# The last FFN products of a retention and maxout kernel by one level of Strassen's algorithm, from the second token tile on

## The chip, the cores and the metric

The kernel runs on one core of a Trainium2 chip. The metric is device time in microseconds (us) of one execution; medians are of several executions. The profile is of one execution; times in it count from its span's start. The engines are TensorE (PE for matmuls, PEld for its weight loads), VectorE (DVE), ScalarE (ACT), GpSimd (POOL) and SyncE (SP, which here issues the transfers). PSUM is the memory that TensorE writes its results to. The granted clock is the share of TensorE's full clock that the chip's throttle let through.

## The reference

```python
scores = (1 / sqrt(D)) * q @ k.transpose(0, 1, 3, 2)     # 8 batches, 8 heads, 576 tokens, D = 64
out    = (scores * Dmat) @ v                              # Dmat: decay gamma**(i-j), lower triangle
x      = out.transpose(0, 2, 1, 3).reshape(4608, 512)
h      = maximum(maximum(x @ w1, x @ w2), x @ w3)         # 512 -> 768
return (h @ w_out).astype(float32)                        # 768 -> 512
```

Everything is computed in float32; the weights come as float64 and are converted on the chip.

## The kernel before

Tokens go in nine tiles of 512. While the feed-forward of tile t runs, the attention of tile t+1 is computed in four chunks of three steps each (transposes, scores, values); a step stands between any two pieces of feed-forward work. A tile has nine "up" units, for three pairs fp of 128-column blocks of h and three weight matrices i, and then the last layer, called "down". From tile 1 on the up units already use one level of Strassen's algorithm (Winograd's form): seven products of half size in place of eight, with sums of the blocks made beforehand. Down is plain:

```python
def up(t, h, fp, i):                        # seven products, 4 instructions each
    product(1, x, True);  p1 = kept("p1", x)            # kept: ScalarE copy out of PSUM
    ...
    product(5, x, False)
    nc.vector.tensor_tensor(c22, x[:], p7[:], op=ALU.add)      # L343, frees bank x for product 3
    ...
    product(3, x, False)
    ...                                                        # i > 0:
        nc.vector.tensor_tensor(h[:, f1, lo], h[:, f1, lo], x[:], op=ALU.max)        # L354
        nc.vector.tensor_tensor(h[:, f0, :], h[:, f0, :], ..., op=ALU.max)           # L355

def down(t, h, m):
    ps = ps_y.tile([P, DM], FP32, tag="y", name="down")
    for fb in range(NF):                                       # NF = 6
        nc.tensor.matmul(ps[:], lhsT=h[:, fb, m * P:(m + 1) * P], rhs=w_sb["out", fb][:],
                         start=(fb == 0), stop=(fb == NF - 1))
    osb = opool.tile([P, DM], FP32, tag="osb", name="osb")
    nc.scalar.copy(osb[:], ps[:])
    nc.sync.dma_start(out[...], osb[:])

def ffn(t):
    for n, (fp, i) in enumerate(units):
        ...                                                    # up (tile 0: plain)
            if t == 1:
                weight_sums(n + 2)                             # sums of w1..w3, made during tile 1
        yield                                                  # an attention step runs here
    for m in range(NT // P):                                   # 4 row blocks
        down(t, h, m)
        ...
```

## Time and profile before

| | before |
|---|---|
| time, median of 3 runs | 861.55 us (860.62 to 861.91) |
| span of the profiled run | 857.7 us |
| mean granted TensorE clock | 0.998 |
| TensorE matmuls busy | 844.4 us, 98% |
| VectorE busy | 393.6 us, 46% |
| GpSimd busy | 143.3 us, 17% |

TensorE is the bound; VectorE is idle for more than half of the span.

### The profile page before, as it was taken

Reading aid. Unit: us, or ns where it says so; the run is one execution under the profiler, and the core shown is the slowest. Engines: PE = TensorE matmul, PEld = TensorE weight load, DVE = VectorE, ACT = ScalarE, POOL = GpSimd, SP = SyncE. Lnnn points to the kernel's source line nnn. Section 1 sums busy time; section 2 is a strip of 40 time slices with the busy share of each in tenths; the row PEclk is TensorE's granted clock in tenths of the full one; section 3 lists DMA queues with packets and bytes.
Section 4 is the critical chain, followed back from the end, with each engine's and each line's share of the span. In section 5 each row is a group of like instructions: output and inputs, shape, how many; then the busy total and the mean of one; then the engine's idle time right before and its main releaser. Section 6 shows DMA issues by size and latency. Waiting matters only on the chain.

```text
span 857.7 us, 11778 instructions
## 1 busy us (share of the span) xinstructions
PE 844.4 (98%) x4320; PEld 614.0 (72%) x4320; DVE 393.6 (46%) x705; ACT 171.4 (20%) x367; POOL 143.3 (17%) x128
## 2 busy tenths in 40 slices
PE   7999989999999999999999999999999999999998
PEld 5645546887588758885788668875888588857883
DVE  4899945654244523444254335442544235432330
ACT  2565631111111102110111111111111011101211
POOL 3534423221210120102011111101111102100000
PEclk9999999999999999999999999999999999999999
DMA  9655531334133323332233213341333223200001
GB/s 245 173 151 160 181 70 43 55 57 85 43 54 56 55 66 66 54 56 61 47 64 68 57 49 56 55 85 45 56 56 54 66 52 66 44 26 24 1 1 49
DMA packets 228409, 59.01 MB, mean 69 GB/s; under 512 B 213504, under 2 KB 222720, under 8 KB 228352
## 3 DMA queue, kind: packets, MB, share of 16 engines
q1 hardware_dynamic: 227920, 57.74, 29.9%
q8 instruction: 34, 0.56, 0.3%
q10 hardware_dynamic: 432, 0.53, 0.2%
q14 instruction: 23, 0.19, 0.1%
HBM read 48.76 MB, written 9.44 MB: 68 GB/s over the span
## 4 chain that ended last, share of the span: by engine, by line
PE 87%; DVE 6%; ACT 4%; issue 1%; DMA 1%; SPq 1%; POOL 0%; DVEq 0%; ACTq 0%
PE x L315 29%; PE down L361 21%; PE z L315 14%; PE y L315 7%; PE s L178 4%; PE o L208 4%; PE o L213 3%; PE kv L189 3%; ACT expo L267 2%; ACT expo L271 1%; DVE expo L275 1%; DVE expo L264 1%; DVE h L375 1%; DVE st L181 1%; DMA kraw<-in_k_dram 1%
## 5 line engine op out<-in xcount | busy, mean ns | idle before, releaser
L361 PE MATMUL down<-wout,h 128*128 128x512 f32 x432 | 190.7, 594 | 3.0 <-POOL wout L278 3.0
L361 PEld LDWEIGHTS down<-wout,h 128*128 128x128 f32 x432 | 80.6, 190 | 95.9 <-issue 90.6
L315 PE MATMUL x<-S,T 128*128 128x256 f32 x576 | 147.9, 379 | 0.0
L148 POOL TENSOR_TENSOR vd<-vraw,gk 128x512 f32<-128x512 f32 x36 | 38.7, 1076 | 499.5 <-DMA vraw<-in_v_dram 483.6
L315 PEld LDWEIGHTS x<-S,T 128*128 128x128 f32 x576 | 109.1, 190 | 15.4 <-ACT u L320 0.3
L181 DVE TENSOR_TENSOR st<-s,causal 128x512 f32<-128x512 f32 x72 | 46.3, 685 | 65.6 <-PE s L178 65.6
L315 PE MATMUL x<-xT,w 128*128 128x256 f32 x288 | 74.8, 382 | 0.0
L315 PE MATMUL x<-S,w 128*128 128x256 f32 x288 | 74.4, 381 | 0.1
L315 PE MATMUL z<-xT,T 128*128 128x256 f32 x288 | 74.0, 379 | 0.0
L315 PE MATMUL z<-S,w 128*128 128x256 f32 x288 | 73.9, 379 | 0.0
L315 PE MATMUL y<-xT,w 128*128 128x256 f32 x288 | 73.9, 379 | 0.0
L320 ACT COPY p<-x 128x256 f32<-128x256 f32 x72 | 26.8, 373 | 220.8 <-PE x L315 217.8
L343 DVE TENSOR_TENSOR tmp<-x,p 128x256 f32<-128x256 f32 x48 | 20.4, 425 | 104.4 <-PE x L315 104.4
L364 ACT COPY osb<-down 128x512 f32<-128x512 f32 x36 | 21.1, 586 | 219.7 <-PE down L361 212.4
L370 PE MATMUL up<-xT,w 128*128 128x512 f32 x144 | 63.5, 594 | 0.4 <-DVE xT L215 0.4
L315 PEld LDWEIGHTS z<-S,w 128*128 128x128 f32 x288 | 54.7, 190 | 7.4
L315 PEld LDWEIGHTS y<-xT,w 128*128 128x128 f32 x288 | 54.7, 190 | 7.4
L315 PEld LDWEIGHTS z<-xT,T 128*128 128x128 f32 x288 | 54.0, 189 | 8.4 <-ACT p L320 0.3
L315 PEld LDWEIGHTS x<-S,w 128*128 128x128 f32 x288 | 49.4, 189 | 13.4 <-issue 1.3
L315 PEld LDWEIGHTS x<-xT,w 128*128 128x128 f32 x288 | 51.5, 190 | 9.6 <-issue 4.2
L215 DVE TENSOR_TENSOR xT<-o,gq 128x512 f32<-128x512 f32 x36 | 24.8, 690 | 69.7 <-PE o L213 63.8
L370 PEld LDWEIGHTS up<-xT,w 128*128 128x128 f32 x144 | 26.7, 190 | 30.9 <-issue 30.1
(64 smaller groups left out, 867.8 us busy)
## 6 DMA issues: line engine op xcount, KB each, us to landing
bits<-in_moe_w_dram SPq DMA_DIRECT2D x18, 512.0 KB, 3.6
out_dram<-osb SPq DMA_DIRECT2D x36, 256.0 KB, 2.0
kraw<-in_k_dram SPq DMA_DIRECT2D x32, 256.0 KB, 3.0
vraw<-in_v_dram SPq DMA_DIRECT2D x32, 256.0 KB, 3.5
qraw<-in_q_dram SPq DMA_DIRECT2D x448, 16.0 KB, 1.9
kxraw<-in_k_dram SPq DMA_DIRECT2D x448, 16.0 KB, 1.8
bits<-in_moe_w_out_dram SPq DMA_DIRECT2D x6, 512.0 KB, 3.5
qraw<-in_q_dram SPq DMA_DIRECT2D x7, 256.0 KB, 4.6
```

The lines of the kernel that those rows point to most:

```text
L148: nc.gpsimd.tensor_tensor(t[:], raws.pop(("v", g))[:], gk[:].unsqueeze(2).to_broadcast([C, H, D]), op=ALU.mult)
L178: nc.tensor.matmul(s[j][:, p, :], lhsT=kT[r, p, :], rhs=qT[r, p, :], start=True, stop=True)
L181: nc.vector.tensor_tensor(st[:, j], s[j][:], masks[start_of(g)][:].unsqueeze(1).to_broadcast([C, NP, C]), op=ALU.mult)
L189: nc.tensor.matmul(kv[:, p, :], lhsT=pair(kr, p)[r:], rhs=pair(vds[g], p)[r:], start=True, stop=True)
L208: nc.tensor.matmul(o[D * j:D * (j + 1), p, :], lhsT=vr[:, 2 * p + j, :], rhs=st[:, j, p, :], start=(p == 0), stop=(old == 0 and p == NP - ...
L213: nc.tensor.matmul(o[:, p, :old], lhsT=sd[:, p, :], rhs=qT[:, p, :old], start=False, stop=(p == NP - 1), skip_group_check=True)
L215: nc.vector.tensor_tensor(xT[t][:, :, i * C:(i + 1) * C], o[:], gq[:], op=ALU.mult)
L315: nc.tensor.matmul(out[:], lhsT=w[:, d * P:(d + 1) * P], rhs=xS[t][n][:, d, :], start=first and d == 0, stop=d == 1, skip_group_check=True)
L320: nc.scalar.copy(c[:], src[:])
L361: nc.tensor.matmul(ps[:], lhsT=h[:, fb, m * P:(m + 1) * P], rhs=w_sb["out", fb][:], start=(fb == 0), stop=(fb == NF - 1))
L364: nc.scalar.copy(osb[:], ps[:])
L370: nc.tensor.matmul(ps[:], lhsT=w_sb[i, fb][:, dc * P:(dc + 1) * P], rhs=xT[t][:, dc, :], start=(dc == 0), stop=(dc == NDC - 1))
```

## The change

The last layer gets the same scheme. From tile 1 on it is seven products of (2 row blocks) × (3 pairs fp) matmuls with 256 columns. The sums of w_out are made once (`sums_of_outs`), behind unit 2 of tile 1. The sums of h are made per pair fp (`sums_of_hidden`) behind the unit that finishes the pair, which is unit 2, 5 or 8. The memory of the weight conversion is freed for them. The diff, cut to its core:

```diff
+    def sums_of_outs():
+        while_converting.close()
+        ...
+        nc.vector.tensor_tensor(t1, b12, b11, op=ALU.subtract)      # 128 x 768
+        nc.vector.tensor_tensor(t2, b22, t1, op=ALU.subtract)
+        nc.gpsimd.tensor_tensor(b12, b22, b12, op=ALU.subtract)
+        nc.gpsimd.tensor_tensor(t4, b21, t2, op=ALU.subtract)
+    def sums_of_hidden(h, fp):
+        ...
+        nc.vector.tensor_tensor(s1, a21, a22, op=ALU.add)           # 128 x 256
+        nc.vector.tensor_tensor(s2, s1, a11, op=ALU.subtract)
+        nc.gpsimd.tensor_tensor(s3, a11, a21, op=ALU.subtract)
+        nc.gpsimd.tensor_tensor(s4, a12, s2, op=ALU.subtract)
+    def downs(t, h):
+        def product(n, out, first):
+            for m in range(NM):                                     # NM = 2
+                for fp in range(NF // 2):                           # 3
+                    nc.tensor.matmul(out[:, m, :], lhsT=hS[n](fp)[:, m * P:(m + 1) * P],
+                                     rhs=late["T"][n][:, fp, :], start=..., stop=...)
+        ...                                     # products 1, 2, 6, 7, 5, 4, 3 as in up
@@ ffn
                 if t == 1:
                     weight_sums(n + 2)
+                if i == 2:
+                    if t == 1 and fp == 0:
+                        sums_of_outs()
+                    sums_of_hidden(h, fp)
             yield
+        if t == 0: ...                          # plain down
+        else:
+            for n, _ in enumerate(downs(t, h)): ...
```

## The prediction

> **What bounds the kernel now.** I read the page first: engine shares, then the chain that ended last, then the costliest groups.
>
> ```profile
> PE 844.4 (98%) x4320; PEld 614.0 (72%) x4320; DVE 393.6 (46%) x705; ACT 171.4 (20%) x367; POOL 143.3 (17%) x128
> PE 87%; DVE 6%; ACT 4%; issue 1%; DMA 1%; SPq 1%; POOL 0%; DVEq 0%; ACTq 0%
> L361 PE MATMUL down<-wout,h 128*128 128x512 f32 x432 | 190.7, 594 | 3.0 <-POOL wout L278 3.0
> L361 PEld LDWEIGHTS down<-wout,h 128*128 128x128 f32 x432 | 80.6, 190 | 95.9 <-issue 90.6
> L315 PE MATMUL x<-S,T 128*128 128x256 f32 x576 | 147.9, 379 | 0.0
> ```
>
> TensorE is busy 98% of the span and is 87% of the chain, so a TensorE instruction taken out of tiles 1 to 8 shortens the kernel one for one, unless a new wait eats it. The busy times of groups can't be added (pipelined matmuls of neighbouring groups overlap), so the cost of a matmul must come from starts. Two stretches of the last tile, where no attention is left, give it. First the chain, then the timeline around the last product of the last unit:
>
> ```profile
> 833.59 20.61 PE down L361 x48
> ```
>
> ```profile
> 831.70 1.03 PE L315 MATMUL z<-xT,T 128*128 128x256 f32 x4
> ...
> 832.56 1.03 PE L315 MATMUL x<-S,w 128*128 128x256 f32 x4
> ...
> 833.42 20.76 PE L361 MATMUL down<-wout,h 128*128 128x512 f32 x48
> ...
> 833.63 0.42 DVE L354 TENSOR_TENSOR h<-h,x 128x256 f32<-128x256 f32 x1
> ...
> 833.97 0.68 DVE L355 TENSOR_TENSOR h<-h,tmp 128x512 f32<-128x512 f32 x1
> ```
>
> A last-layer ("down") tile is 24 matmuls, which the trace shows as 48 instructions (an fp32 matmul is two), 20.61/48 = 0.429 us each at 512 columns. A Strassen product of the up layers (4 instructions of 256 columns) starts 0.86 us after the one before it: 832.56 − 831.70 = 0.86, 833.42 − 832.56 = 0.86, so 0.215 to 0.216 us each. Half the columns cost half the time: **the narrow matmul has almost no fixed cost**, since the weight load (190 ns) just fits under it. That is why Strassen pays at all here.
>
> The same lines show something that helps the old order and will not help the new one. The maximum that finishes the last pair of blocks of h (L355) ends at 833.97 + 0.68 = 834.65, 1.23 us after the first down matmul started. The old loop does not need that pair before its ninth instruction, 8 × 0.429 = 3.43 us in.
>
> **What the Trainium skill says.** (1) "TensorE: Matmul & The Clock Gate", Back-to-back issue gap: N/2.4 + 2.5 ns warm, 216 ns at 512 and 109 ns at 256. The trace has twice that for fp32 (429 and 216 ns), in the same proportion; I use the trace. (2) The same page, LDWEIGHTS: P/1.2, 107 ns for 128 columns; the trace says 190 ns, which leaves only 26 ns under a 216 ns matmul. (3) "SBUF — State Buffer", Who interferes with whom: a VectorE instruction with two SBUF inputs contends with a GpSimd instruction that reads SBUF. The trace agrees: L290 (256 columns) takes 0.41 us alone and 0.94 us beside GpSimd. (4) "Perfetto Trace Analysis", Tensor Engine Instruction: ends of TensorE instructions are estimates; hence my use of starts.
>
> **The change part by part.**
>
> *Matmuls.* Seven products × 2 row blocks × 3 pairs = 42 matmuls, 84 instructions of 256 columns. An up unit (28 such) repeats every 6.04 us in the last tile, so 84 take 3 × 6.04 = 18.12 us against 20.61 us. The gain is **2.49 us a tile, 19.9 us over eight tiles (2.3% of 861.55)**. Tile 0 keeps the old products. The weight loads rise from 48 to 84 a tile and stay hidden.
>
> *Evictions.* Out go four ScalarE copies of 512 (586 ns each, L364). In come six copies of 256 (373 ns), one of 512 on ScalarE, and six additions of 256 on VectorE (425 ns). A product now lasts 12 × 0.216 = 2.59 us, and each bank is next written one product later; two copies (0.75 us) or two additions (0.85 us) end well inside that. The up layers do the same with 0.86 us products and hardly ever wait. **Cost on the path: zero.** The output is the same bytes in four transfers; the tail (copy, transfer) I take as at most 0.3 us longer.
>
> *First product waits for h.* Product 1 takes fp = 0, 1, 2 in turn for its first row block, so it needs the last pair after 4 instructions: 4 × 0.216 = 0.86 us, not 3.43. In the last tile it would load at once but for L355: that ends at 834.65, the load then starts some 0.05 us later and its matmul 0.11 us after that (as in the wait shown below), at 834.81, where 833.42 + 0.86 = 834.28 was its turn. **0.53 us lost.** In the other tiles only two VectorE transposes stand between the last unit and product 1, nothing on TensorE, so the loss is the same: 8 × 0.53 = 4.2 us.
>
> *Sums of h.* Per pair of blocks: two VectorE and two GpSimd operations of 256 columns, three times a tile, right behind L355. They are not on TensorE, but VectorE works in order, and behind units 2 and 5 it then has the attention transposes (0.70 + 0.66) before it may serve unit 3 or 6. The trace has one case where exactly this queue stopped TensorE (tile 1, unit 3, where weight sums take the place of the new ones):
>
> ```profile
> 161.01 1.22 DVE L355 TENSOR_TENSOR h<-h,tmp 128x512 f32<-128x512 f32 x1
> 162.15 0.94 DVE L290 TENSOR_TENSOR T<-w,w 128x256 f32<-128x256 f32 x1
> 163.12 0.83 DVE L291 TENSOR_TENSOR T<-w,T 128x256 f32<-128x256 f32 x1
> 163.88 0.70 DVE L159 STREAM_TRANSPOSE kT<-kxraw 128x512 f32<-128x512 f32 x1
> 164.51 0.66 DVE L159 STREAM_TRANSPOSE qT<-qraw 128x512 f32<-128x512 f32 x1
> 165.10 0.38 DVE L333 TENSOR_TENSOR h<-y,p 128x256 f32<-128x256 f32 x1
> 165.41 0.40 DVE L343 TENSOR_TENSOR h<-x,p 128x256 f32<-128x256 f32 x1
> ...
> 165.86 0.73 PEld L315 LDWEIGHTS x<-S,w 128*128 128x128 f32 x4 [0.46 <-DVE h L343]
> ```
>
> L343 must empty x before product 3 writes it. How much room it has elsewhere is its idle time before it. In tile 7:
>
> ```profile
> 711.01 1.42 DVE L355 TENSOR_TENSOR h<-h,tmp 128x512 f32<-128x512 f32 x1
> ...
> 714.50 0.42 DVE L343 TENSOR_TENSOR h<-x,p 128x256 f32<-128x256 f32 x1 [0.55 <-PE x L315]
> ```
>
> Over tiles 2 to 7 that room in unit 3 is 1.84, 1.09, 1.16, 1.15, 0.94 and 0.55 us, and in unit 6 always 1.84 (1.01 in tile 1). It is small where a value scaling on GpSimd (L148, L195) lands on L355. My estimate for the new pair of sums is between 0.42 + 0.42 alone and 0.94 + 0.83 contended: 1.4 us. Beyond the room that leaves 0, 0.3, 0.25, 0.25, 0.45, 0.85 in unit 3 and 0.4 in unit 6 of tile 1: 2.5 us in all. The last tile has no transposes and loses none.
>
> *Sums of w_out, once.* They enter that same full queue in tile 1 before unit 3, where there is no room left. VectorE does two of 768 columns: from 0.41 us at 256 and 0.68 us at 512, about 0.95 us alone, the second about 1.9 us beside GpSimd. Adding the first sums of h (1.7 us contended) gives 4.5 us. **All of it should stop TensorE: 4.5 us.**
>
> *Sum.* 861.55 − 19.9 + 4.2 + 2.5 + 4.5 + 0.3 = 853.15, say **853.2 us**, 1.0% less.
>
> **The rivals.** (a) *Nothing is lost*: VectorE is only 46% busy, the sums vanish in idle time, all 19.9 us arrive: 841.7 us, faster by 2.3%. For it: the up layers run this scheme with almost no wait. Against it: the h dependency of product 1 is visible in starts, and VectorE's spare time is not where it is needed. (b) *VectorE's queue becomes the bound behind units 2, 5 and the down phase*: contention doubles all sums and GpSimd's own delays the decayed values and states. Were each of some 24 places to lose 0.8 us, the gain would be gone: about 861 us. The room of 1.84 us in unit 6 speaks against it. (c) *The weight load becomes the bound*: at 190 of 216 ns, if loads of the new layout slipped to 230 ns, 672 instructions × 14 ns = 9 us more, 862. The up layers already load from SBUF tiles of the same form at 216 ns, so I doubt it. (d) *The output transfers on the one in-order queue hold back the loads of q and k*: they are issued in the same order, and the last one now comes earlier, so no.
>
> **Range and chances.** The matmul gain is firm to about 0.5 us; the losses could be 4 to 18 us. So 848.0 to 858.5 us eight times in ten. Faster by 2% needs under about 844.5, thus losses under 3 us, less than product 1's wait alone: 5%. Slower by 2% would need 37 us of new waits: 1%.
>
> **What would show it.** The page should have no L361 down rows but tile 0's 48, and new product rows of 256 columns with starts 0.216 us apart. The waits of TensorE and its loads should list the last maximum of h ahead of product 1 (eight times about half a microsecond), and L343's counterpart ahead of product 3 in unit 3 of tile 1 (4 to 5 us) and, smaller, of tiles 3 to 7. VectorE busy should rise by some 50 to 60 us, ScalarE by some 4 (8 × (6 × 0.373 + 0.586 − 4 × 0.586) = 3.8). The prediction is wrong if product 1 doesn't wait, if the sums run without contention, or if starts in the new products are further apart than 0.216 us.

## The result

| | before | changed |
|---|---|---|
| time, median of 4 runs | 861.73 us (860.62 to 862.91) | 858.55 us (857.14 to 859.74) |
| ratio | | 0.9962 (0.9942 to 0.9982) |
| span of the profiled run | 857.7 us | 855.4 us |
| mean granted TensorE clock, profiled run | 0.998 | 0.991 |

A ratio is the mean time of one kernel's runs over that of the other's runs of the same rounds, so it is not quite the ratio of the medians quoted. The change is faster by 0.4%, within 2%, where 1.0% had been expected (853.2 us, in a range up to 858.5).

The page of the changed kernel, the engine shares, the granted clock in 40 slices and the chain that ended last by engine:

```profile
PE 831.4 (97%) x4608; PEld 669.8 (78%) x4608; DVE 448.2 (52%) x803; ACT 172.8 (20%) x391; POOL 189.4 (22%) x178
...
PEclk9999999989999999999999999999999999999999
...
PE 79%; DVE 8%; SPq 5%; ACT 4%; issue 3%; DMA 1%; POOL 0%; DVEq 0%
```

TensorE is busy 13 us less, but the span is only 2.3 us shorter. TensorE's share of the chain is down from 87% to 79%, and one slice of the clock row, the ninth (171 to 192 us), is no longer a 9. That slice lies in tile 1. (SyncE's 5% of the chain is an effect of how it is followed back: from transposes that queue behind the sums it goes to a transfer. VectorE's instructions stand back to back there, so no transfer held it up, and in e5 below the share is 1%.) To see where the expected gain went, compare starts of the same matmuls in the two traces:

| stretch | before | changed | difference |
|---|---|---|---|
| tile 1: product 3 of unit 2 to product 3 of unit 3 | 6.26 us | 13.00 us | +6.74 |
| tile 1: product 3 of unit 3 to product 1 of unit 4 | 3.15 us | 5.88 us | +2.73 |
| tile 1: product 3 of unit 2 to first down matmul | 45.15 us | 55.25 us | +10.1 |
| first down matmul of tile 1 to the end of the span | 652.95 us | 640.48 us | −12.5 |

So from the down phase of tile 1 on, the change earns 12.5 us, near what was expected, and **one stretch of tile 1 gives 10.1 us of it back**. Here it is, in the timeline of the changed kernel (columns: start, us, engine, line, operation; in brackets how long the engine had stood idle and what ended it). L322 and L323 are VectorE's sums of h, L312 and L313 its sums of w_out, L314 and L315 GpSimd's; L434 was L343 before, and L446 was L355.

```profile
164.01 1.48 DVE L312 TENSOR_TENSOR To<-w_out 128x768 f32<-128x768 f32 x1
...
165.52 1.36 DVE L313 TENSOR_TENSOR To<-w_out,To 128x768 f32<-128x768 f32 x1
166.03 2.51 POOL L314 TENSOR_TENSOR w_out<-w_out 128x768 f32<-128x768 f32 x1
...
166.81 2.02 DVE L322 TENSOR_TENSOR H<-h 128x256 f32<-128x256 f32 x1
168.51 1.98 POOL L315 TENSOR_TENSOR To<-w_out,To 128x768 f32<-128x768 f32 x1
168.86 1.90 DVE L323 TENSOR_TENSOR H<-H,h 128x256 f32<-128x256 f32 x1
...
172.22 0.40 DVE L434 TENSOR_TENSOR h<-x,p 128x256 f32<-128x256 f32 x1
...
172.67 2.08 PE L406 MATMUL x<-S,w 128*128 128x256 f32 x4 [6.80 <-DVE h L434]
...
174.68 2.08 PE L181 MATMUL s<-qT,kT 64*128 64x128 f32 x16
...
178.55 1.07 PE L406 MATMUL x<-xT,w 128*128 128x256 f32 x4
```

Two things are to be seen. First, VectorE's two sums of 256 columns took 2.02 and 1.90 us, and they end 0.29 and 0.27 us after the GpSimd instruction that ran beside each (166.81 + 2.02 = 168.83 against 166.03 + 2.51 = 168.54, and so on): each sat through GpSimd's. The same pair usually takes 0.42 and 0.83 us. VectorE is in order, so the transposes and then L434 come late, and TensorE stands for 6.80 us. Second, what TensorE does after the wait is slow as well: four matmuls take 2.08 us on record instead of 1.13, sixteen score matmuls 2.08 instead of 1.16. The same three groups in the kernel before:

```profile
165.86 1.13 PE L315 MATMUL x<-S,w 128*128 128x256 f32 x4
166.92 1.16 PE L178 MATMUL s<-qT,kT 64*128 64x128 f32 x16
...
169.01 1.03 PE L315 MATMUL x<-xT,w 128*128 128x256 f32 x4
```

The granted clock of the stretch from 170 to 180 us is 0.57. Asked in steps of 1 us, the trace has it at one half from 168.4 us, 2.5 us into the wait, to 178.6 us: 10.2 us in all, of which TensorE worked the last 6. (In every kernel here, the one before too, there is one more such fall, of 3.4 us, in tile 0. In the kernel before it begins at 117.3 us, behind waits of 1.10 and 1.90 us for converted weights. It is why the mean there is 0.998 and not 1.)

The other predicted wait, ahead of the last pair in product 1, is there in each of eight tiles (tile 1 shown):

```profile
214.92 1.03 PE L342 MATMUL dx<-w_out,h 128*128 128x256 f32 x4
...
215.46 0.69 DVE L446 TENSOR_TENSOR h<-h,tmp 128x512 f32<-128x512 f32 x1
...
216.20 1.99 PE L342 MATMUL dx<-w_out,h 128*128 128x256 f32 x8 [0.25 <-DVE h L446]
```

The second group's turn was 214.92 + 4 × 0.216 = 215.78. Its record starts with its weight load at 216.20, and the matmul itself 0.11 us later: 0.53 us late.

### The profile page after: what moved, and what is told of

Its sections match the earlier page's. It is cut to its first block, busy times and chain, and to the rows that moved or that the text cites. A ratio compares the mean times of both kernels' runs of the same rounds, so it can differ in the third digit from the quotient of the medians.

```text
span 855.4 us, 12581 instructions
## 1 busy us (share of the span) xinstructions
PE 831.4 (97%) x4608; PEld 669.8 (78%) x4608; DVE 448.2 (52%) x803; ACT 172.8 (20%) x391; POOL 189.4 (22%) x178
## 4 chain that ended last, share of the span: by engine, by line
PE 79%; DVE 8%; SPq 5%; ACT 4%; issue 3%; DMA 1%; POOL 0%; DVEq 0%
PE x L406 26%; PE z L406 12%; PE dx L342 9%; PE y L406 6%; PE dz L342 5%; PE s L181 4%; SPq L141 4%; PE o L211 4%; PE o L216 3%; PE kv L192 3%; PE dy L342 2%; PE down L452 2%; ACT expo L271 2%; ACT expo L275 1%; DVE expo L279 1%
## 5 line engine op out<-in xcount | busy, mean ns | idle before, releaser
L406 PE MATMUL x<-S,w 128*128 128x256 f32 x288 | 76.2, 387 | 8.6 <-DVE h L434 8.5
L434 DVE TENSOR_TENSOR tmp<-x,p 128x256 f32<-128x256 f32 x48 | 20.4, 425 | 104.8 <-PE x L406 104.8
L324 POOL TENSOR_TENSOR H<-h 128x256 f32<-128x256 f32 x24 | 22.7, 947 | 150.3 <-DVE h L446 150.3
L181 PEld LDWEIGHTS s<-qT,kT 64*128 64x128 f32 x576 | 37.2, 198 | 13.9 <-issue 11.4
L424 DVE TENSOR_TENSOR tmp<-y,p 128x256 f32<-128x256 f32 x48 | 20.4, 425 | 51.7 <-PE y L406 51.7
```

The source lines that it names most:

```text
L181: nc.tensor.matmul(s[j][:, p, :], lhsT=kT[r, p, :], rhs=qT[r, p, :], start=True, stop=True)
L406: nc.tensor.matmul(out[:], lhsT=w[:, d * P:(d + 1) * P], rhs=xS[t][n][:, d, :], start=first and d == 0, stop=d == 1, skip_group_check=True)
```

## The experiments

Theory A, formed from the two traces: three separate waits of TensorE ate the gain. They are the one-off sums of w_out in VectorE's full queue (with GpSimd holding VectorE up, and with a clock that falls during the wait), the wait of product 1 for the last pair of h, and the sums of h ahead of the transposes. Rivals: the sums cost the same wherever they stand; the lower clock comes from the denser narrow matmuls; the narrow products are themselves slower than taken. All seven runs gave correct results and were timed in five rounds against the kernel before.

| run | median us | kernel before | ratio (95% interval) |
|---|---|---|---|
| changed kernel | 858.55 | 861.73 | 0.9962 (0.9942 to 0.9982) |
| e1_outs_late | 851.28 | 861.83 | 0.9882 (0.9868 to 0.9896) |
| e2_gpsimd_part_late | 856.71 | 861.83 | 0.9948 (0.9934 to 0.9961) |
| e3_pair_last | 854.33 | 861.83 | 0.9918 (0.9903 to 0.9933) |
| e4_hidden_later | 851.03 | 861.83 | 0.9871 (0.9853 to 0.9889) |
| e5_all_three | 841.41 | 861.34 | 0.9765 (0.9752 to 0.9778) |
| e6_filled_wait | 856.53 | 861.34 | 0.9939 (0.9927 to 0.9951) |
| e7_sums_only | 872.78 | 861.04 | 1.0138 (1.0121 to 1.0155) |

The stretches of tile 1 from the profiled runs, as in the table above:

| run | unit 2 product 3 to unit 3 product 3 | unit 3 product 3 to unit 4 | unit 2 product 3 to first down matmul |
|---|---|---|---|
| before | 6.26 | 3.15 | 45.15 |
| changed | 13.00 | 5.88 | 55.25 |
| e1_outs_late | 8.00 | 3.14 | 47.47 |
| e2_gpsimd_part_late | 10.49 | 5.77 | 52.58 |
| e3_pair_last | 12.94 | 5.88 | 55.22 |
| e4_hidden_later | 9.18 | 4.76 | 49.68 |
| e5_all_three | 6.48 | 3.15 | 45.37 |
| e6_filled_wait | 12.75 | 3.15 | 52.23 |
| e7_sums_only | 12.85 | 5.89 | 55.37 |

e3 and e7 leave the queue of tile 1 as the change made it, and both repeat its delay: it is not a chance of one execution.

### e1_outs_late: the one-off sums behind unit 7

```diff
     def sums_of_outs():
-        nc.vector.tensor_tensor(t1, ...); nc.vector.tensor_tensor(t2, ...)
-        nc.gpsimd.tensor_tensor(b12, ...); nc.gpsimd.tensor_tensor(t4, ...)
+        def rest(): ...                     # the same four
+        late["rest"] = rest
@@ ffn, t == 1
+                    if n == 7:
+                        late["rest"]()
```

> The four one-off sums of w_out move from behind unit 2 of tile 1 to behind unit 7, where no weight sums and no attention transposes stand in VectorE's queue. Theory A (the one-off sums block VectorE's queue, TensorE waits 6.8 us ahead of product 3 of unit 3 and then runs some 3 us at half clock): the first down matmul of tile 1, 10.1 us later than in the kernel before, comes within 2 us of it, the granted clock is back at 0.998, and the time falls by 8 to 9.5 us to about 849 to 850.5. Rival B (the sums cost VectorE and GpSimd the same wherever they stand, the wait only moves to product 3 of unit 8 or to the first down products): a fall of under 3 us. Rival C (the lower clock comes from the denser narrow matmuls, not from the wait): the clock stays near 0.991 and the fall is about 7 us.

Measured: 851.28 us, 7.3 us less than the changed kernel, a little under the expected 8 to 9.5; the first down matmul comes 47.47 − 45.15 = 2.3 us late, not within 2. The time alone would fit rival C too; the clock decides. It is 0.998 in the profiled run and the stretch after unit 3 is 3.14 us again (three of the four executions have 0.998; the slowest, 852.41 us, has 0.996 and no trace). At the new place VectorE's two sums look like this in the timeline:

```profile
201.61 0.95 DVE L314 TENSOR_TENSOR To<-w_out 128x768 f32<-128x768 f32 x1
...
202.59 0.96 DVE L315 TENSOR_TENSOR To<-w_out,To 128x768 f32<-128x768 f32 x1
```

They cost 1.9 us instead of 2.8, and TensorE's list of waits has none for them: the same four instructions, in another place, are free. Rival B falls. So does rival C: the products are as dense as before and the clock is back. What the expectation had overlooked is that the sums of h of pair 0 still stand behind unit 2 among the weight sums, so that unit 3 keeps a delay of 8.00 − 6.26 = 1.74 us.

### e2_gpsimd_part_late: only GpSimd's half moved

```diff
         nc.vector.tensor_tensor(t1, ...); nc.vector.tensor_tensor(t2, ...)
-        nc.gpsimd.tensor_tensor(b12, ...); nc.gpsimd.tensor_tensor(t4, ...)
+        def rest(): ...                     # GpSimd's two, called at n == 7
```

> Only GpSimd's two one-off sums (768 columns, 2.5 and 2.0 us) move to behind unit 7; VectorE's two stay behind unit 2. Theory A1 (VectorE's first two sums of h took 2.0 and 1.9 us instead of 0.42 and 0.83 because GpSimd's two sums held the reads): those two fall to about 0.9 and 0.8 us, TensorE's wait from 6.8 to about 4.3 us, the time by 2.5 us if the clock still drops and up to 5 us if it does not. Rival (the queue is long because of its own VectorE work, contention is a detail): the wait stays above 6 us and the time within 1 us of the changed kernel.

In the timeline, the two sums of h (L326 and L327 here) and the matmul that waited:

```profile
169.39 0.94 DVE L326 TENSOR_TENSOR H<-h 128x256 f32<-128x256 f32 x1
170.37 0.42 DVE L327 TENSOR_TENSOR H<-H,h 128x256 f32<-128x256 f32 x1
...
172.75 2.07 PE L410 MATMUL x<-S,w 128*128 128x256 f32 x4 [4.28 <-DVE h L438]
```

They fall from 3.92 to 1.36 us together, and the wait from 6.80 to 4.28 us: 2.5 us, as expected of theory A1 (of the two sums, the second fell further than expected: to 0.42 us, not 0.8). **GpSimd's two sums made VectorE's two sums of h 2.5 us longer.** The clock still dropped (for 6.8 us, and the stretch after the wait is 5.77 us), and the time fell by 1.8 us. That is under the expected 2.5, but the intervals of the two ratios overlap; the stretches of the trace are the firmer measure here.

### e3_pair_last: the last pair of blocks last in each product

```diff
         def product(n, out, first):
-            for m in range(NM):
-                for fp in range(NF // 2):
+            for fp in range(NF // 2):
+                for m in range(NM):
```

> Down products take fp in the outer loop and the row block in the inner, so that the last pair of blocks of h is needed after 8 instructions of 0.216 us (1.73 us) instead of 4 (0.86 us). Theory A: the maximum that finishes that pair ends 1.23 us after the first down matmul, so the wait of about half a microsecond ahead of product 1 goes in all eight tiles: 4 us less, about 854.5. Rival (TensorE waits the same time a little later in product 1, or the order of writes to the bank costs time): within 1 us of the changed kernel.

Measured: 854.33 us, 4.2 us less, and the wait of product 1 for L446 is gone from the list of waits. The 0.53 us × 8 of the prediction is confirmed, by an edit that swaps two lines.

### e4_hidden_later: the sums of h behind units 3 and 6

```diff
                 if i == 2:
                     ...
-                    sums_of_hidden(h, fp)
+                    if fp == NF // 2 - 1:
+                        sums_of_hidden(h, fp)
+                if n in (3, 6):
+                    sums_of_hidden(h, n // 3 - 1)
```

> The sums of h of pairs 0 and 1 move from behind units 2 and 5 (full queue: maxima, then attention transposes) to behind units 3 and 6, which end without maxima and are followed by attention scores. Theory A: the waits ahead of product 3 of unit 3 in tiles 3 to 7 and of unit 6 in tile 1 (about 2 us together) go, and in tile 1 the wait behind unit 2 falls from 6.8 to about 3 us[...]: 2 + 3.8 + 2.6 = about 8 us less in all, 850. Rival (the sums are cheap, only the one-off sums matter): the tiles after the first gain nothing, and the time falls by what tile 1 gains alone.

Measured: 851.03 us, 7.5 us less. The waits of matmuls ahead of product 3 in tiles 2 to 7 are gone but for one of 0.17 us (tile 7, unit 0), which the changed kernel has too, and in tile 1 one of 2.95 us is left. One part of the expectation missed: I had taken a wait of 3 us to be too short for the clock to drop (the 2.6 us of the sum are the clock's). In the profiled execution it did drop, for 3.4 us:

```profile
171.58 1.96 PE L406 MATMUL x<-S,w 128*128 128x256 f32 x4 [2.95 <-DVE h L434]
...
173.47 1.95 PE L181 MATMUL s<-qT,kT 64*128 64x128 f32 x16
```

The five timed runs fall into two kinds: 848.43 and 849.09 us with a mean clock of 0.998, and 851.03 to 852.20 us with 0.993 to 0.996. That looks as if the drop came in three of five executions and cost some 2 to 3 us, but only one of them has a trace, and why the same wait should let the clock drop in some executions only is not shown.

### e5_all_three: the three edits together

The edits of e1, e3 and e4 in one kernel.

> The three edits together: one-off sums behind unit 7, last pair of h last in each down product, sums of h of pairs 0 and 1 behind units 3 and 6. Theory A (three separate waits on TensorE, which add up): from 858.55, 7.3 less for the first, 4.2 less for the second, and for the third the 5.6 us of waits ahead of product 3 that the first run alone left: about 841.5, faster than the kernel before by 2.3 to 2.4%, close to the full worth of the matmuls, 861.7 - 19.9 = 841.8. Rival (the waits share a cause and the gains overlap, or the sums reappear as waits elsewhere): 846 or more.

Measured: **841.41 us, 0.9765 of the kernel before, faster by 2.35%**, as theory A had it and against the rival's 846. It beats both kernels. (The gains of e1 and e4 alone, 7.3 and 7.5 us, don't add up, since both shorten the same wait of tile 1.) The engine shares and the chain on its page:

```profile
PE 826.3 (98%) x4608; PEld 670.2 (80%) x4608; DVE 440.8 (52%) x803; ACT 172.8 (21%) x391; POOL 184.7 (22%) x178
...
PE 86%; DVE 6%; ACT 4%; issue 2%; DMA 1%; SPq 1%; POOL 0%; DVEq 0%
```

TensorE is back at 98% busy and 86% of the chain, with the same number of instructions as in the changed kernel. The list of TensorE's waits holds no wait of a matmul for VectorE in tiles 1 to 8 above 0.4 us (of weight loads, one of 0.55 us).

### e6_filled_wait: work put into the wait

```diff
+        if t == 1 and fp == 1 and i == 0:
+            fill = ps_r.tile([P, NP, C], FP32, tag="r", name="fill")
+            for _ in range(15):
+                nc.tensor.matmul(fill[...], lhsT=ident[:], rhs=xT[t][:, 0, 0:NH], start=True, stop=True)
         product(3, x, False)
```

> The changed kernel with 15 useless matmuls of 256 columns (30 instructions, 6.5 us) put ahead of product 3 of unit 3 in tile 1, into a PSUM bank that nobody reads: TensorE works through the wait in place of idling. Theory A (the idle wait of 6.8 us lets the clock fall to half, and that costs 2.7 us after the wait): product 3 starts when it did, but the stretch from product 3 of unit 3 to product 1 of unit 4 goes from 5.9 back to 3.15 us, the granted clock from 0.991 to 0.998, and the time falls by about 2.7 us although work was added. Rival (that stretch is long for another reason, such as late scores or VectorE's backlog): no gain, or up to 6.5 us slower.

In the timeline, the filling, product 3, the scores after it and the next unit:

```profile
167.30 6.64 PE L444 MATMUL fill<-xT,ident 128*128 128x256 f32 x30
...
174.00 1.13 PE L406 MATMUL x<-S,w 128*128 128x256 f32 x4
...
175.06 1.16 PE L181 MATMUL s<-qT,kT 64*128 64x128 f32 x16
...
177.15 1.03 PE L406 MATMUL x<-xT,w 128*128 128x256 f32 x4
```

Product 3 comes as late as in the changed kernel (12.75 us after unit 2's, against 13.00), but what follows takes 3.15 us instead of 5.88, exactly as before the change. The kernel does 30 more matmul instructions and takes 2.0 us less by the medians (2.7 expected). The intervals of the two ratios just overlap, so the time alone would not settle it. The clock does: all six executions have 0.997 or 0.998, all four of the changed kernel 0.991 to 0.994. So the slow stretch came from TensorE's idling, and from nothing in the work that follows.

### e7_sums_only: the sums without the products

```diff
-        nc.gpsimd.tensor_tensor(b12, b22, b12, op=ALU.subtract)
+        nc.gpsimd.tensor_tensor(t3, b22, b12, op=ALU.subtract)     # w_out kept as it is
@@ ffn
-        if t == 0:
+        if True:                                                   # plain down in all tiles
```

> The changed kernel with the old last-layer products in all tiles: all sums of w_out and of h are made where the change makes them (one of them into a tile of its own, so that w_out stays as it was), but nobody reads them; the result stays right. It measures what the sums cost without the products' gain and without product 1's wait. Theory A: tile 1 loses its 10 us again and tiles 2 to 7 some 2 to 3 us before product 3 of units 3 and 6, so 861.5 + 10 + 2.5 = about 874, and the difference to the changed kernel, some 15.5 us, is the matmuls' 19.9 less product 1's 4.2. Rival (the narrow down products lose time themselves, for instance by their weight loads, and the sums cost less): 868 or less.

Measured: 872.78 us, 11.7 us over the kernel before. The difference to the changed kernel, by the ratios, is (1.0138 − 0.9962) × 861.5 = 15.2 us, against some 15.5 expected. The sums alone cost the 11.7 us, and the narrow products give what their instruction count says.

## Why the prediction was wrong

**The step that failed is "Sums of w_out, once": "All of it should stop TensorE: 4.5 us".** The mechanism was right: the sums enter VectorE's queue where it has no room, L343's counterpart comes late, and product 3 of unit 3 waits. The size was not. With the rest of tile 1 it cost 10.1 us:

- *The queue.* It was 6.74 us late, 2.2 us more than put down. Of the sum's terms, the two sums of w_out held together (1.48 + 1.36 = 2.84 us for the 0.95 + 1.9 predicted), though by luck: the first was not alone, and both met GpSimd's weight sums (L299, L300), not its sums of w_out. The first pair of sums of h did not: it took 2.02 + 1.90 = 3.92 us for the 1.7 predicted. I had scaled contention from instructions of 256 columns beside others of 256. Here each met a GpSimd instruction of 768 columns and sat it out. The Trainium skill says just this ("SBUF — State Buffer", SBUF: two separate sides: whichever instruction starts first has the shared pair of ports for the whole instruction, and the other blocks fully); I had cited the page and still used a factor.
- *The clock.* 2.73 us were lost after the wait, a term the prediction didn't have. The skill's "TensorE: Matmul & The Clock Gate", What's actually happening, states that the clock goes to half after an idle window of about 3.4 us. A predicted wait of 4.5 us was already long enough to ask for it. The trace (0.57 granted from 170 to 180 us) and e6 agree that idling brings the fall; on the length of the idling they differ (see the last section).

Together these are 4.9 us, and 853.2 + 4.9 = 858.1, against 858.55 measured. Most of the rest is the 0.5 us of the sums of h below.

The other steps, in the prediction's order:

- *Matmuls, 2.49 us a tile.* Right. A product of 12 instructions repeats every 2.59 us in the last tile, so seven take 18.13 us for 18.12 predicted; e5 delivers 19.9 us (861.34 − 841.41).
- *Evictions free.* Right: none of the new copies or additions is on TensorE's list of waits. ScalarE grew by 1.4 us rather than 3.8, for two copies in a row take 0.65 us, not 0.75.
- *Product 1 waits 0.53 us, eight times.* Right, by starts and by e3.
- *Sums of h, 2.5 us.* Nearly right in sum, not in place. The weight loads ahead of product 3 waited 0.88, 0.88, 0.29, 0.64, 0.21 and 0.29 us in unit 3 of tiles 2 to 7, and 0.72 in unit 6 of tile 1. Some 0.13 us of each is no loss: in tile 1, unit 6, the scores came 0.59 us late. That leaves 3.0 us. The room seen before was no guide to a single tile (tile 7, with 0.55 us of room, lost little, tile 2, with 1.84, lost most); in tile 2 a scaling on GpSimd (L198) now ran beside the first sum, which took 1.38 us. Why it ran there is not shown.
- *The rivals.* Loads of the weights did not become a bound, nor did the output transfers. Rival (a), nothing lost, is what e5 reached, 841.4 for 841.7 us, once the order of the work had been mended.

## What to carry to other kernels

When sums are to be hidden behind a full TensorE, ask not how idle VectorE is on average but what stands in its in-order queue at that very place, and put them where the next instruction TensorE depends on is farthest away; the same four instructions cost TensorE 7 us in one place and nothing in another. When a wait of some microseconds is predicted, add what the clock loses after it. In a loop over a sum, take last the operand that is ready last.

## What the Trainium skill lacked or had wrong

- "TensorE: Matmul & The Clock Gate", Back-to-back issue gap: the formula gives 216 ns at 512 columns and 109 ns at 256, and the page has none for float32. Float32 takes twice that per instruction (429 and 216 ns, weight loads included), and a float32 matmul is two instructions in the trace. That makes four times in all; the four passes of true float32 stand on another page, "FP8 and Floating Point Precision", not here.
- The same page, LDWEIGHTS: 107 ns by its formula for 128 columns; 190 ns in the trace for float32.
- The same page, What's actually happening: it asks for an idle window of about 3.4 us. Shorter waits sufficed here: in e4 the clock fell by half after a wait recorded as 2.95 us for matmuls (3.35 us for weight loads), and in tile 0 of every kernel behind two waits with matmuls between them (1.10 and 1.90 us in the kernel before). A single wait of 1.79 us in tile 1 of e1 left the stretch after it at full speed. The falls of tile 1 lasted 3.4, 6.8 and 10.2 us in e4, e2 and the changed kernel.
- The same page, Terms: it puts the loss at the time spent at the lower clock times the share of the clock that is missing, which would be 10.2 × 0.5 = 5.1 us in the changed kernel. The runs show 2.7 us, for TensorE stood waiting during the first 4.3 us of the fall.
- "SBUF — State Buffer", Who interferes with whom: right, but without durations for float32. VectorE's sums of 256 columns took 0.42 us alone, 0.83 to 0.95 us beside a GpSimd instruction of 256 columns, and 1.90 to 2.02 us beside one of 768.
